# Another stored table for the order of issue in an attention and channel-mix kernel

## The chip, the cores and the metric

The kernel runs on one core of a Trainium2 chip. The metric is the device time of one execution in microseconds (us), the lower the better. A core has five engines that run beside each other, each with its own list of instructions, taken strictly in order: TensorE (PE, matrix products), VectorE (DVE), ScalarE (ACT), GpSimd (POOL), and SyncE (SP), which here issues all DMAs.

## What is computed

The reference is attention over pooled queries, followed by a channel mix; 8 batches, 8 heads, 1152 keys, 576 pooled queries, head size 64.

```
q_pool = q.reshape(B, H, S // 2, 2, D).mean(axis=3)
scores = q_pool @ k^T / sqrt(D); attn = softmax(scores); x = attn @ v    # x: (8, 576, 512)
x_prev = x moved by one position
xk = mu_k * x + (1 - mu_k) * x_prev;  xr = mu_r * x + (1 - mu_r) * x_prev
k = relu(xk @ w_k); v = (k * k) @ w_v; r = sigmoid(xr @ w_r); out = r * v
```

## The kernel before, in words

**Attention.** The 64 heads (8 batches of 8) are taken one after another, each in 6 blocks of 96 queries, 384 blocks in all (`block`, called at L808). A block uses one of three PSUM buffers `s0` to `s2` in turn and goes back and forth between the engines. PE computes 9 scores matmuls of 96 columns (L490, in two steps of 4 and 5). DVE takes the maximum over key chunks (L497). PE transposes it (L500), DVE takes the maximum again (L503), PE adds the correction (L505), ACT writes it into a row of the queries' low part (L508). PE runs 9 second scores matmuls on top (L514, two steps). ACT takes the exponential of all into `pf` (L520), and POOL cuts the low parts out of it (L523). With that the buffer is free for the block three further on. Where all queries of a stretch are there, `window` multiplies the weights with V: 9 pairs of hi matmuls (L549 and L551, 65 and 64 columns, in three steps) and 9 lo matmuls (L556, 65 columns, two steps) into one buffer `a`. After the head's last window DVE and ACT take `a` out (L573 to L580). For each head `prep` loads K and V, splits them into high and low halves (L433, L438, L457, L460, L463) and turns K by DMA (L449, L452); every second head `queries` does the like for two heads' queries (L388 to L416).

**Weights.** In the first 8 heads, batch 0, the weights of the channel mix, which come as 64-bit floats, are loaded (L630) and unpacked in 20 pieces by ACT (L638, L641, L653), DVE (L643, L645) and POOL (L654).

**Channel mix.** As soon as a batch's heads are through, `ff` runs over tiles of 256 positions, 18 in all: DVE and ACT mix x with its shifted copy (L686, L689, L695, POOL L697), and PE does 96 product matmuls of 256 columns and 72 of 512 columns for a tile (all at L717), with ACT (L744 to L770), POOL (L748) and DVE (L772, L781) between them and a store at the end (L784). Batch 0 and its successor's heads overlap: the products of a batch are issued between the blocks of the next one.

**The order.** No loop above issues anything at once. Each step is handed to `op` (`Issue.add`, L167) with its engine, a duration, and the buffers it reads and writes; one step can hold several matmuls. There are 5946 PE steps, 1590 for DVE, 1803 for ACT, 932 for POOL and 498 DMAs. `run` (L228) then reads the stored table `TURNS` (L50 to L141), one list for each engine, which says at each place how many of the engine's steps not yet issued are passed over. That alone sets the order on each engine:

```
for e in ENGINES:
    left = [n for n in range(len(ops)) if eng[n] == e]
    while left:
        ...
        order.append(left.pop(k + step))
```

`follow` (L194) plays these lists with the durations and the latencies `LAT` (L153), and the steps are put into the program by the times that come out; that sets how instructions of different engines stand against each other in the program, and nothing on one engine. The last lines of the kernel (L816 to L824) pin each engine's order.

Of the kernel before, what the change touches and what calls it, by code (L numbers as in the profile page):

```python
# [17 lines left out]
U8 = mybir.dt.uint8  # L18
# [4 lines left out]
P = 128  # L23
# [27 lines left out]
    "c-n<}349e*miMW8Rqxf?>+Nfjm*i#N6S9%8Z(#?CKxn~$ASjy(LR3Iha2v&_Ev+r?TQg2iI||y4wnDeltu`*LG#$j1j$?~}iX!}Qx${4_0y^K<-|"  # L51
    "sv3y{cPxU(WxWa~D!=I%%04B8B3V$k<3#)nqsr35SBQs7mCI$NgbHk<ah-l1b$9nl7IU9w!+NCy{QD<|W<lBMn6mX@=&}9Cp+0aR)VrL$ezp(}-$"
    "b-L5$(YPT7B%1^59wrQ%a#<fsL)AX38sV<uu4oAuDFdUwUL$NEmn<Dmr-EWUL?3xw{J0cq8JM&1>HO+`*kwrBk{E_rTG{2^j63%rPUWX%&%mL&M*"
    "&QjnJsx%;Q89&WPTj8S31^Bl)#g+S@;R?B7{iwu_mR`(bjG~Ngi|q;7#U8(88bX_d(2_?7EwgcC%eOAx5tpltrg_Q><$#|BVD)IVqQ*ecp~w*q54"
    "#NUY_9$k;CB*J9MvIr%*;_O~vdO8Lc3e;k@LH>Nc{eo=9%4l^c2UReL0tFan&H(Ce_vsx@g(*ikP<^YV1NU)Q7D2ju0P=zd&vs9rmTIVZV7s7Ke3"
    "5#y$7#Pf?em6KzUO~WMD)WT6)HNq>JDk>`LDk|!0I%{id5NxZiwpEptRa91tEGsLs*{Z6mY?YO^ilWlehN7aPnxbMjTh@lMvXm`?qrzbYxw)BKP+"
    "m5hn@jnWsmb7xN6DOIGL<YyrZUN{B;`?VI)`%7luAXTiD;Cf6p2tcNr?ph0g9TY8KR&czj)Mdl8+)D3Q;&n!9c+2B)8#o8!opC>{o=!3$ulUxzRv"
    "m)ubkf^0Snm$xr7c!{IcAK=D`zRRvK^GLcMB+%)xwmKTotLSdiJNB&UE7mcGW5sw;DT`tq*@_2o2m)os6{p9oc(+Zg1W5;wGy2Bv5-R1Ub9*@_f8"
    "7^15%hjqmooIsHlk#|ydZp%axg)L;w=3W>41_b!xLspnE*b?ka~K9W?BIS-p*@qI$yB4Y8CA_y)hrK8K}yNX!x-k|<mM#O2@u8Od2yn2C8Y?%lua"
    "h$@i@g0l8U4;Vy0$BqgoR+cx|>iGOIgPzlnZ%lnHJJ6WIYwHyY`jGR27|7)FQD(XiSu>NJNJ4RpB-Cj!AvjfQb9nhZvDy9`c<w&sJcY<8Q?hLQ|8"  # L60
# [189 lines left out]
def kernel(  # L250
# [219 lines left out]
    def block(n, j, i, t):  # L470
# [14 lines left out]
        def grid(c0, c1):  # L485
            return cols(c0, c1).rearrange("p (c q) -> p c q", q=QN)
# [368 lines left out]
```

## Time and profile before

| | us |
|---|---|
| median of 3 runs | 1116.58 (1115.95 to 1116.6) |
| the profiled execution, whole | 1115.82 |
| its span, first to last instruction | 1114.0 |
| busy: PE, DVE, ACT, POOL | 1077.0, 893.2, 842.0, 805.1 |

The profile is of one execution. Its span is 1.8 us shorter than that execution's own time, which is 0.8 us under the median. A busy PE in the profile is not PE at its peak, since matmuls overlap; the distance between the starts of two matmuls tells how fast it really goes. In the tables of windows the stretches are in us from the span's start, and PEclk is the share of full clock granted to TensorE, 1.00 for 2.4 GHz.

### The profile page before, as it was taken

How to read it: one execution, taken by the hardware profiler on the slowest of the kernel's cores; microseconds unless marked ns; L12 is line 12 of the kernel's file. 1: busy time of each engine (PE TensorE's matmuls, PEld its weight loads, DVE VectorE, ACT ScalarE, POOL GpSimd, SP SyncE). 2: the span in 40 equal slices, each digit the busy share in tenths (PEclk: the TensorE clock that was granted, in tenths of full speed). 3: DMA queues.
4: the chain of work that ended last, by engine and by line, in shares of the span. 5: the costliest groups of instructions: out<-in, count | busy, mean ns of one | idle time of the engine just before them, and what ended most of it. 6: DMA issues, size and time to landing. Idle time of an engine off the chain costs nothing.

```text
span 1114.0 us, 44713 instructions
## 1 busy us (share of the span) xinstructions
PE 1077.0 (97%) x18802; PEld 889.3 (80%) x18802; DVE 893.2 (80%) x1606; ACT 842.0 (76%) x1804; POOL 805.1 (72%) x940
## 2 busy tenths in 40 slices
PE   6888799999999999999999999999999999999998
PEld 5777687988788897988787888889797979787564
DVE  7999988898898898988787878787888889774321
ACT  6899987877878787878777786878777778765653
POOL 4778888877858787777777786868688777765431
PEclk9999999999999999999999999999999999999999
DMA  9999547675557654556455655565756354510000
GB/s 250 212 199 227 132 120 150 138 167 117 134 115 133 137 119 100 140 132 139 118 100 132 114 127 113 123 141 102 134 114 143 94 124 104 87 40 23 19 20 29
DMA packets 258153, 135.35 MB, mean 121 GB/s; under 512 B 193440, under 2 KB 230304, under 8 KB 257952
## 3 DMA queue, kind: packets, MB, share of 16 engines
q1 hardware_dynamic: 257952, 132.50, 54.4%
q8 instruction: 147, 2.41, 0.9%
q14 instruction: 54, 0.44, 0.1%
HBM read 67.11 MB, written 9.44 MB: 69 GB/s over the span
## 4 chain that ended last, share of the span: by engine, by line
PE 68%; DVE 1%; POOL 0%; DMA 0%; ACT 0%; issue 0%; POOLq 0%; DVEq 0%
PE f L717 28%; PE s L514 9%; PE s L490 9%; PE a L549 5%; PE a L551 5%; PE s L717 4%; PE a L556 4%; PE a L717 2%; PE s L500 1%; PE s L505 1%; DVE mx L497 0%; DMA kr<-in_k_dram 0%; DVE xr L689 0%; POOL pl L523 0%; DVE xk L689 0%
## 5 line engine op out<-in xcount | busy, mean ns | idle before, releaser
L497 DVE TENSOR_REDUCE mx<-s 128x96 f16<-128x864 f32 x384 | 399.6, 1052 | 83.5 <-PE s L490 43.2
L523 POOL TENSOR_SCALAR pl<-pf 128x864 f16<-128x864 uint16 (+1 forms) x384 | 332.8, 867 | 147.3 <-ACT pf L520 113.6
L520 ACT ACTIVATE pf<-s 128x864 int32<-128x864 f32 x384 | 335.2, 886 | 94.5 <-PE s L514 69.8
L549 PE MATMUL a<-vt,pf 128*128 128x65 f16 x2880 | 241.4, 194 | 0.6 <-DVE xb L580 0.4
L551 PE MATMUL a<-vt,pf 128*128 128x64 f16 x2880 | 241.8, 194 | 0.0
L490 PE MATMUL s<-qT,ks 128*128 128x96 f16 x3456 | 224.0, 208 | 10.1 <-ACT pf L520 8.1
L514 PE MATMUL s<-qT,ks 128*128 128x96 f16 x3456 | 215.8, 207 | 4.4 <-ACT qT L508 4.2
L490 PEld LDWEIGHTS <-ks 128*128 128x128 f16 x3456 | 184.4, 99 | 33.7 <-issue 12.2
L549 PEld LDWEIGHTS <-pf 128*128 128x128 f16 x2880 | 204.8, 98 | 5.1
L551 PEld LDWEIGHTS <-pf 128*128 128x128 f16 x2880 | 195.4, 98 | 8.2 <-issue 0.9
L514 PEld LDWEIGHTS <-ks 128*128 128x128 f16 x3456 | 179.7, 98 | 24.2 <-issue 5.5
L508 ACT ACTIVATE qT<-s 1x96 f16<-1x96 f32 x384 | 87.9, 233 | 77.1 <-PE s L505 73.2
L503 DVE TENSOR_REDUCE mb<-s 128x1 f16<-128x128 f32 x384 | 108.7, 286 | 37.1 <-PE s L500 32.9
L717 PE MATMUL f<-xhk,wk_hi 128*128 128x256 f16 x496 | 135.1, 272 | 0.5 <-DVE ex L645 0.5
L717 PE MATMUL f<-xlk,wk_hi 128*128 128x256 f16 x496 | 135.2, 272 | 0.1
L717 PE MATMUL f<-xhk,wk_lo 128*128 128x256 f16 x496 | 135.2, 272 | 0.0
L556 PE MATMUL a<-vb,pl 128*128 128x65 f16 x2304 | 126.6, 193 | 0.4 <-POOL pl L523 0.4
L717 PEld LDWEIGHTS <-wk_hi 128*128 128x128 f16 x1152 | 105.7, 98 | 14.9 <-issue 0.6
L556 PEld LDWEIGHTS <-pl 128*128 128x128 f16 x2304 | 101.0, 98 | 6.9 <-POOL pl L523 0.7
L748 POOL TENSOR_TENSOR gl<-g 128x512 f16<-128x512 f32 x72 | 77.0, 1071 | 40.4 <-ACT g L746 37.4
L438 POOL TENSOR_TENSOR kn<-kr,kn 128x320 f16<-128x320 f32 (+1 forms) x126 | 97.1, 785 | 5.9 <-ACT kn L433 1.8
L717 PE MATMUL f<-wv_lo,g 128*128 128x512 f16 x240 | 90.9, 379 | 0.0
(112 smaller groups left out, 2153.2 us busy)
## 6 DMA issues: line engine op xcount, KB each, us to landing
kr<-in_k_dram SPq DMA_DIRECT2D x64, 288.0 KB, 3.3
vr<-in_v_dram SPq DMA_DIRECT2D x64, 288.0 KB, 3.1
qr<-in_q_dram SPq DMA_DIRECT2D x32, 320.0 KB, 3.6
ks<-ks SPq DMA_DIRECT2D x64, 144.0 KB, 2.7
out_dram<-em SPq DMA_DIRECT2D x36, 256.0 KB, 2.3
qr<-in_q_dram SPq DMA_DIRECT2D x32, 256.0 KB, 3.3
st<-in_moe_w_k_dram SPq DMA_DIRECT2D x4, 512.0 KB, 6.0
xt<-in_moe_w_k_dram SPq DMA_DIRECT2D x4, 512.0 KB, 6.0
```

Source lines behind the costliest of these rows:

```text
L438: lambda cs=cs, en=nc.vector if ve else nc.gpsimd: en.tensor_tensor(kn[i][:, cs, D:P], kr[i][:, cs], kn[i][:, cs, 0:D], op=ALU.subtract),
L490: nc.tensor.matmul(cols(c, c + 1), ks1[hp][:, c, :], qhi, start=(c == c0), stop=False, skip_group_check=True)
L497: op("DVE", 0.967, lambda: nc.vector.tensor_reduce(mxz[:, P - QN:P], grid(0, NC).rearrange("p c q -> p q c"), axis=AX.X, op=ALU.max), r=[( ...
L503: op("DVE", 0.199, lambda: nc.vector.tensor_reduce(mbz, s[:, 0:P], axis=AX.X, op=ALU.max), r=[("s", z)], w=[("mb", z)], key=t + O_MAX)
L508: op("ACT", 0.15, lambda: nc.scalar.activation(qlo[0:1], s[0:1, 0:QN], AF.Prelu, scale=1.0 - EPS, alpha=(1.0 + EPS) / (1.0 - EPS)), r=[("s ...
L514: nc.tensor.matmul(cols(c, c + 1), ks2[hp][:, c, :], qlo, start=False, stop=True, skip_group_check=True)
L520: op("ACT", NC * QN / 1200 + 0.051, lambda: nc.scalar.activation(pf[:, :, HALF + rows.start:HALF + rows.stop], grid(0, NC), AF.Exp, bias=S ...
L523: op("POOL", NC * (r1 - r0) / 1000 + 0.066, lambda: nc.gpsimd.tensor_scalar(to, half(pf, U16, 0)[:, :, HALF + r0:HALF + r1], LO, 1.0, op0= ...
L549: nc.tensor.matmul(a_b[:, a0:a0 + VN], half(pf, F16, 1)[:, c, his], vt[jv][:, c, D:D + VN], start=(w == 0 and c == 0), stop=False, skip_gr ...
L551: nc.tensor.matmul(a_b[:, a0:a0 + D], half(pf, F16, 1)[:, c, his], vt[jv][:, c, 0:D], start=False, stop=(side and c == NC - 1), skip_group ...
L556: nc.tensor.matmul(a_b[:, a0:a0 + VN], pl[:, c, rows], vb[jv][:, c, 0:VN], start=False, stop=(c == NC - 1), skip_group_check=True)
L717: nc.tensor.matmul(ps, terms[i][0], terms[i][1], start=(first and i == 0), stop=(i == last), skip_group_check=True)
```

## The change

All of `TURNS` is replaced (91 lines by 91, the first and last of them below), and with it some durations and latencies that `follow` uses. The steps themselves, their instructions, shapes and buffers, are the same.

```diff
 TURNS = (
-    "c-n<}349e*miMW8Rqxf?>+Nfjm*i#N6S9%8Z(#?CKxn~$ASjy(LR3Iha2v&_Ev+r?TQg2iI||y4wnDeltu`*LG#$j1j$?~}iX!}Qx${4_0y^K<-|"
...
-    "Pm$l~ZnQ2xYE{{u{8&C>"
+    "c-nP(34j#E)&J|Bo|&GW`@VN)cV;h^z3*jNcDa|E-30_W)&oIZJOE{pO92nOAjTsq#&{dA_$dJ;p8=!MXi#H70Z*btO+W%7f<&$V@6{~I_x<y|n("
...
+    "KCPRPwui1{Pl<`=gcuCNqf0D%QaGtjuz3JEsxW)_uHEGs1YboGMXNmDQYiA?+{KWU%;2f_-X-T"
 )
...
-           ("ACT", "POOL"): 0.18, ("DVE", "POOL"): 0.155, ("POOL", "PE"): 0.11, ("ACT", "DVE"): 0.142,
-           ("DVE", "ACT"): 0.128, ("DVE", "DVE"): 0.12, ("ACT", "ACT"): 0.13, ("POOL", "POOL"): 0.13}
+           ("ACT", "POOL"): 0.18, ("DVE", "POOL"): 0.155, ("POOL", "PE"): 0.04, ("ACT", "DVE"): 0.142,
+           ("DVE", "ACT"): 0.128, ("DVE", "DVE"): 0.12, ("ACT", "ACT"): 0.13, ("POOL", "POOL"): 0.07}
...
-            op("DVE" if ve else "POOL", nn / 960 + 0.069 if ve else nn * 0.0020 + 0.11,
+            op("DVE" if ve else "POOL", nn / 960 + 0.069 if ve else nn * 0.0019 + 0.19,
...
-            op("PE", (c1 - c0) * 0.043, lambda c0=c0, c1=c1: scores(c0, c1),
+            op("PE", (c1 - c0) * 0.0425, lambda c0=c0, c1=c1: scores(c0, c1),
...
-            op("POOL", NC * (r1 - r0) / 1000 + 0.066, lambda: nc.gpsimd.tensor_scalar(
+            op("POOL", 0.93 if buf == ("pside",) else NC * (r1 - r0) / 1200 + 0.273, lambda: nc.gpsimd.tensor_scalar(
...
-            op("PE", 3 * 0.0595, lambda c0=c0: hi(c0, c0 + 3),
+            op("PE", 3 * 0.06, lambda c0=c0: hi(c0, c0 + 3),
...
-            op("PE", (c1 - c0) * 0.030, lambda c0=c0, c1=c1: lo(c0, c1),
+            op("PE", (c1 - c0) * 0.0322, lambda c0=c0, c1=c1: lo(c0, c1),
...
```

The other edited durations are of the same kind: the V low copy (0.67 to 0.75), the maximum (0.967 to 0.974), the transpose of the maximum (0.054 to 0.057), the correction (0.05 to 0.047), and the POOL and DVE steps of the turn, the weights and the mix.

Both tables can be read back to lists of steps. How they stand against each other (places moved, old list to new):

| engine | steps | on another place | mean move |
|---|---|---|---|
| PE | 5946 | 5573 | 9.2 |
| DVE | 1590 | 1443 | 5.4 |
| ACT | 1803 | 1591 | 4.6 |
| POOL | 932 | 707 | 2.0 |
| SP (DMA) | 498 | 388 | 2.2 |

And the number of steps in the lists up to and with a block's last step of a kind, old and new (blocks counted from 0 over all heads; 48 is the first of batch 1):

| block | PE, to L514 | of these products, in matmuls | DVE, to L503 | ACT, to L520 |
|---|---|---|---|---|
| 41 | 407, 400 | 0, 0 | 173, 177 | 187, 193 |
| 47 | 472, 459 | 0, 0 | 200, 199 | 214, 220 |
| 53 | 519, 551 | 6, 42 | 223, 226 | 244, 256 |
| 59 | 626, 650 | 82, 105 | 252, 252 | 278, 286 |
| 65 | 710, 757 | 124, 154 | 271, 283 | 306, 321 |
| 95 | 1157, 1150 | 312, 312 | 397, 393 | 438, 433 |

The first steps of ACT after the table load, old: mb, K cast 0, K cast 5, query cast 0, K copy, query cast 5, query copy (L412); new: mb, K cast 5, K cast 0, query cast 0, K copy, V copy 0, query copy (L412).

## Rows read from the trace of the kernel before

**Rows 1.** The page's first part: busy time in us, share and instructions of each engine.

```profile
PE 1077.0 (97%) x18802; PEld 889.3 (80%) x18802; DVE 893.2 (80%) x1606; ACT 842.0 (76%) x1804; POOL 805.1 (72%) x940
```

**Rows 2.** From the chain of waits that ended last, pieces in order of time: start in us, us, what; x is the number of matmuls run one behind the other.

```profile
487.98 0.77 PE s L514 x18
...
528.27 2.62 PE f L717 x24
...
539.75 2.59 PE f L717 x12
```

**Rows 3.** From the timeline of PE about 22.3 us: start in us, us of one, line and operation; the first and the last of twelve.

```profile
22.14 0.19 PE L549 MATMUL a<-vt,pf 128*128 128x65 f16 x1
...
22.47 0.19 PE L551 MATMUL a<-vt,pf 128*128 128x64 f16 x1
```

**Rows 4.** Groups of instructions by line, over the span: the count, busy us and mean ns of one, idle before them.

```profile
L551 PE MATMUL a<-vt,pf 128*128 128x64 f16 x2880 | 241.8, 194 | 0.0
L549 PE MATMUL a<-vt,pf 128*128 128x65 f16 x2880 | 241.4, 194 | 0.6 <-DVE xb L580 0.4 <-ACT xt L608 0.2
L490 PE MATMUL s<-qT,ks 128*128 128x96 f16 x3456 | 224.0, 208 | 10.1 <-ACT pf L520 8.1 <-ACT qT L412 1.7
L514 PE MATMUL s<-qT,ks 128*128 128x96 f16 x3456 | 215.8, 207 | 4.4 <-ACT qT L508 4.2
...
L556 PE MATMUL a<-vb,pl 128*128 128x65 f16 x2304 | 126.6, 193 | 0.4 <-POOL pl L523 0.4
```

**Rows 5.** Windows by stage: from:to, its length, busy us (x instructions) of PE, weight loads, DVE, ACT and POOL, then granted clock, DMA share, GB/s.

```profile
12.00:40.00 28.00, 23.27 (x450) 21.59 (x450) 22.80 (x45) 20.30 (x41) 16.34 (x20) 0.94 1.06 240
40.00:130.00 90.00, 73.14 (x1589) 65.39 (x1587) 86.31 (x165) 81.68 (x174) 70.78 (x83) 0.96 0.88 201
130.00:150.00 20.00, 17.72 (x328) 15.54 (x328) 18.29 (x31) 17.08 (x41) 17.02 (x22) 1.00 0.53 138
150.00:1080.00 930.00, 927.93 (x16217) 765.28 (x16215) 752.68 (x1336) 703.77 (x1515) 690.73 (x800) 1.00 0.52 112
1080.00:1114.00 34.00, 30.26 (x183) 17.71 (x181) 5.24 (x8) 11.72 (x20) 4.98 (x6) 0.97 0.08 31
```

**Rows 6.** The end of the chain of waits.

```profile
1110.30 0.69 DVE em L781
```

**Rows 7.** Timeline of ACT at the start.

```profile
7.29 0.63 ACT L391 ACTIVATE qn<-qs 128x512 f16<-128x512 f32 x1
7.82 0.68 ACT L412 COPY qT<-s 128x640 f16<-128x640 f16 x1
...
9.06 0.78 ACT L457 ACTIVATE vt<-vr 128x320 f16<-128x320 f32 x2
```

**Rows 8.** Groups of instructions of DVE and of ACT in 12:130, with what ended the idle time before them.

```profile
L497 DVE TENSOR_REDUCE mx<-s 128x96 f16<-128x864 f32 x50 | 51.7, 1049 | 4.8 <-PE s L490 3.0 <-ACT qn L391 0.8 <-ACT pf L520 0.4
L503 DVE TENSOR_REDUCE mb<-s 128x1 f16<-128x128 f32 x50 | 13.9, 284 | 2.4 <-PE s L500 2.3
...
L508 ACT ACTIVATE qT<-s 1x96 f16<-1x96 f32 x51 | 11.2, 231 | 5.6 <-PE s L505 5.4
```

**Rows 9.** Timeline of PE and of ACT about 13 us: one buffer's second scores, its exponential, and the scores that follow in it; in brackets the idle time before and what ended it.

```profile
12.81 0.91 PE L514 MATMUL s<-qT,ks 128*128 128x96 f16 x9
13.52 0.59 PE L505 MATMUL s<-negi,mb 128*128 128x96 f16 x2
14.70 0.88 PE L490 MATMUL s<-qT,ks 128*128 128x96 f16 x9 [0.59 <-ACT pf L520]
...
13.76 0.89 ACT L520 ACTIVATE pf<-s 128x864 int32<-128x864 f32 x1 [1.47 <-PE s L514]
```

**Rows 10.** Waits of PE in 135:1114, all of them: who waited for whom, us in total, times, longest.

```profile
PE s L514 <- ACT qT L508: 0.7, 2, 0.4
PE s L490 <- ACT pf L520: 0.6, 2, 0.4
PE s L505 <- DVE mb L503: 0.5, 2, 0.3
PE a L549 <- DVE xb L580: 0.4, 2, 0.2
PE a L556 <- POOL pl L523: 0.2, 1, 0.2
PE s L500 <- DVE mx L497: 0.2, 1, 0.2
```

**Rows 11.** Groups of the V subtraction in 12:130.

```profile
L460 DVE SCALAR_TENSOR_TENSOR vt<-vr,vt 128x320 f16<-128x320 f32 x8 | 4.4, 553 | 0.0
...
L460 DVE SCALAR_TENSOR_TENSOR vt<-vr,vt 128x256 f16<-128x256 f32 x8 | 3.2, 416 | 0.0
```

**Rows 12.** The same over the span.

```profile
L460 DVE SCALAR_TENSOR_TENSOR vt<-vr,vt 128x320 f16<-128x320 f32 x64 | 48.4, 756 | 0.0
...
L460 DVE SCALAR_TENSOR_TENSOR vt<-vr,vt 128x256 f16<-128x256 f32 x64 | 42.3, 662 | 0.0
```

**Rows 13.** Windows of 10 us, columns as in group 5.

```profile
30.00:40.00 10.00, 8.15 (x163) 7.55 (x163) 8.14 (x17) 8.31 (x17) 7.54 (x8) 0.83 1.01 235
50.00:60.00 10.00, 8.12 (x190) 7.22 (x188) 9.59 (x22) 8.46 (x20) 7.38 (x10) 1.00 1.06 275
110.00:120.00 10.00, 7.50 (x146) 6.90 (x143) 8.99 (x18) 8.02 (x17) 7.75 (x9) 0.83 0.92 197
```

More of the change, by code (lines that the diff above doesn't have):

```diff
@@ L56 @@
[L56 to L60, printed above, removed]
@@ new lines @@
+    "pbUuCA(A^?vW@E>g*?YN-TKEI|t8noOjsF`qve@cC2}_+8$xi+oN$Ig#uJPJV|^C#%Cw7OTZVHqyvMq?kytC=OjWljiVixMR0#Ufmk9+O&w9TxN?"
+    "&*EEwiK$=x^YBqCFQ%!0h5YjcXro}a6NeNs1R^6&ALB(RTP*}6rJQjz`60mBhM7Ds}LtI<uXG1|Xg^b^<#k8PmvZ-X%@pQ<cD^|r!A&b|dyDgf<Z"
+    "#HWd@_PMdi`i_BQUd*}VHJ-C&05l>g`yZoglq;<*lAOAg(6_X7xh}Kx*aT1*zWUzS4T2wv4l0VL({^k6!RV-XMx#c(o7-B(QPhW4`y^#wWJ(D-KO"
+    "hg51>m2X?cEG+X!1UO*8WH!WJu;&CZb7L@reg=5l36Fruq2JR1ZXR;xW=WlnvD#p=bAaZ5-}K-lazC(Y(Co;1{;3SQ--QC+pF0Semr(I6S<$F5<("
+    "7K=t27F5$zmDf@sCI!pIx$+96@<x=@mkungEiJ7st*Wl5tgNgUXEK$Ql$4l|ic5-%icEt|s9`D{U@A$c)0uRJaHQ3Il_)1&K$%PdrPGN-9>sGhCp"
@@ new lines @@
+    "RaSOjDHd^7B$D3RAc+UKq+`qO(FF3I;<#3I+xf`36Oz5!?+0f<X#E%6u-b%jM=ve*gmJBQJRjx7#ob2WtC~$VzTY#AUdg7N^5vhv-4_NYBNjYKde"
+    "#9w$;G(O4uB0ZX~jSWYr0sU*lB^ZWhba3t*WCW7RNdcEO@$E>A%W^_Vo%y6L#!|t#fe#2GmQr#Gai=0lyL3WE_Sa|7hNrv4B8HNoL?$#kfE=;m+7"
+    ";QuBMv+m(#aN3P&FaKxq6R9L7y)AnUy#k@GMP+vJJ6%rY^vU>+aM*XxkxS4)l31_4wTBt$w?&Ccp{#OQ$FRS@=}z_jpTrxcqB&AR5X$kP7)PIi6U"
+    "W2hX_*{2zdM+k4JMy0`71~)5t?^uZr=5C&MTzP;I1>Zgo)-lVwDVPMgg(p?|F4LDPmBWrk7G$~+jl&32B>rg6Dlvm0T%G1V|M6hM>!9lMrg#^$r3"
+    "RhDxeHcLagJe{AHr>0WKCzAz9HJwi7Q#vm{o{HzjS+7tmk5c7Pg@TD-Njw=(C=|u2_$h!z^Z8<0$Qw4hG$)bYTT$urs-A&7RW{6e+HNSolG8$VtP"
@@ L462, in prep @@
                r=[("vr", i), ("vt", j, c0)], w=[("vtl", j, c0)], key=key + 4, port=True)
-        op("POOL", 0.67, lambda: nc.gpsimd.tensor_scalar(
+        op("POOL", 0.75, lambda: nc.gpsimd.tensor_scalar(
             vb[j][:, :, 0:D], vr[i], SV, VLO, op0=ALU.mult, op1=ALU.mult),
@@ L493, in block @@
         for c0, c1 in BK:
-            op("PE", (c1 - c0) * 0.043, lambda c0=c0, c1=c1: scores(c0, c1),
+            op("PE", (c1 - c0) * 0.0425, lambda c0=c0, c1=c1: scores(c0, c1),
                r=[("ks1", hp, c) for c in (0, 5) if c < c1 and (c0 < 5 or c)] + kh, w=[("s", z)], key=t)
-        op("DVE", 0.967, lambda: nc.vector.tensor_reduce(mxz[:, P - QN:P], grid(0, NC).rearrange("p c q -> p q c"),
+        op("DVE", 0.974, lambda: nc.vector.tensor_reduce(mxz[:, P - QN:P], grid(0, NC).rearrange("p c q -> p q c"),
                                                          axis=AX.X, op=ALU.max),
            r=[("s", z)], w=[("mx", z)], key=t)
-        op("PE", 0.054, lambda: nc.tensor.matmul(s[:, 0:P], mxz, identb, start=False, stop=False,
+        op("PE", 0.057, lambda: nc.tensor.matmul(s[:, 0:P], mxz, identb, start=False, stop=False,
                                                  skip_group_check=True),
@@ L504, in block @@
            r=[("s", z)], w=[("mb", z)], key=t + O_MAX)
-        op("PE", 0.05, lambda: nc.tensor.matmul(s[:, 0:QN], mbz.broadcast_to([P, P]),
+        op("PE", 0.047, lambda: nc.tensor.matmul(s[:, 0:QN], mbz.broadcast_to([P, P]),
                                                  negi[:, P - QN:P], start=False, stop=False, skip_group_check=True),
@@ L517, in block @@
         for c0, c1 in BK:
[L518 removed]
+            op("PE", (c1 - c0) * 0.0425, lambda c0=c0, c1=c1: scores2(c0, c1),
                r=[("ks2", hp)] + kl, w=[("s", z)], key=t + O_EXP)
@@ L588, in window @@
                r=[("xb", 0), ("xb", 1)], w=[("xbh",), *old[0]], key=t + O_TURN)
-            op("POOL", NW * P * 0.0019 + 0.09, lambda: nc.gpsimd.tensor_tensor(xbl, xz.rearrange(flat), xbh, op=ALU.subtract),
+            op("POOL", NW * P * 0.0019 + 0.2, lambda: nc.gpsimd.tensor_tensor(xbl, xz.rearrange(flat), xbh, op=ALU.subtract),
                r=[("xb", 0), ("xb", 1), ("xbh",)], w=[("xbl",), *old[0]], key=t + O_TURN)
@@ L593, in window @@
                    r=[(kx,)], w=[(kx, "t"), *old[1]], key=t + O_TURN, tail=1.6)
-            op("POOL", TQ * 0.0019 + 0.09, lambda: nc.gpsimd.tensor_tensor(
+            op("POOL", TQ * 0.0019 + 0.2, lambda: nc.gpsimd.tensor_tensor(
                 xt[b % 3][:, g, 1:1 + TQ], xth[:, HALF:], xtl[:, HALF:], op=ALU.add),
@@ L653, in weights @@
                 op("ACT", 0.52, lambda hi=hi, e=e: nc.scalar.copy(hi, e), r=[ke], w=[("w", n, c, f)], key=key)
-                op("POOL", 1.13, lambda lo=lo, e=e, hi=hi: nc.gpsimd.tensor_tensor(lo, e, hi, op=ALU.subtract),
+                op("POOL", 1.18, lambda lo=lo, e=e, hi=hi: nc.gpsimd.tensor_tensor(lo, e, hi, op=ALU.subtract),
                    r=[ke, ("w", n, c, f)], w=[("wl", n, c, f)], key=key)
@@ L688, in mix @@
    r=xk + [("omu", w)], w=[("tmp", z)], key=key + c * dk)
-                op("DVE", ln / 960 + 0.069, lambda x=x, s0=s0, ln=ln, o0=o0, z=z, c=c: nc.vector.scalar_tensor_tensor(
+                op("DVE", ln / 960 + 0.13, lambda x=x, s0=s0, ln=ln, o0=o0, z=z, c=c: nc.vector.scalar_tensor_tensor(
                     xm[w][:, c, o0:o0 + ln], x[:, c, s0 + 1:s0 + 1 + ln], m[:, c:c + 1], tmp[z][:, 0:ln],
@@ L696, in mix @@
                    r=[("x", w, c, False), ("x", w, c, True)], w=[("xh", c)], key=key + c * dk)
-            op("POOL", n * 0.0019 + 0.09, lambda c=c: nc.gpsimd.tensor_tensor(
+            op("POOL", n * 0.0019 + 0.2, lambda c=c: nc.gpsimd.tensor_tensor(
                 xl[w][:, c, 0:n], xm[w][:, c, 0:n], hi[:, c, 0:n], op=ALU.subtract),
@@ L747, in ff @@
                 g32[:, f2, 0:n], r32[z][:, :, 0:n], AF.Square), r=[("r32", z)], w=[("g", f0)], key=key + 1)
-            op("POOL", 2 * n * 0.0018 + 0.1, lambda f2=f2: nc.gpsimd.tensor_tensor(
+            op("POOL", 2 * n * 0.0018 + 0.14, lambda f2=f2: nc.gpsimd.tensor_tensor(
                 gl[:, f2, 0:n], g32[:, f2, 0:n], gh[:, f2, 0:n], op=ALU.subtract),
```

162 lines of the change are left out of this document (78 added, 84 removed).

## The prediction

> **What bounds the kernel now.** First the page's first line [rows 1]: TensorE (PE) is busy 1077.0 of 1114.0 us, VectorE (DVE), ScalarE (ACT) and GpSimd (POOL) 72 to 80%. A busy PE may still be waiting inside, so the second step is its bare work, from the distance between starts in the chain of work and in the timeline at full clock. Eighteen scores matmuls take 0.77 us, 0.0428 each; twenty-four 256-column products 2.62, 0.109 each; twelve 512-column products 2.59, 0.216 each [rows 2]; a 65-column matmul starts 0.030 after the one before (11 distances from 22.14 to 22.47) [rows 3]. Counts times these: 3456 + 3456 scores 295.8; 2880 + 2880 + 2304 window matmuls 241.9 [rows 4]; 18 tiles x 96 products of 256 columns 188.4 and 18 x 72 of 512 columns 279.9; 384 max transposes (128 columns) and 384 corrections (96), by columns from the scores, 38; 3 for transposes. The sum is 1047 us. No order can go below that with its start and end, so all that a new order can touch is some 67 us.
>
> The windows by stage tell where they lie [rows 5]. In 150:1080 PE is busy 927.9 of 930. In 12:150 it is busy 114.1 of 138. In 40:130 DVE is busy 86.3 of 90 and ACT 81.7, PE 73.1: here DVE sets the pace, because batch 0 has no channel-mix products yet to fill PE, and the weights are unpacked on DVE and ACT beside its 48 blocks. From 150 on PE sets the pace. A new order gains where PE comes sooner to its full stage, and loses where it makes PE wait after that. The tail is fixed: the last gate product runs on DVE for 0.69 us from 1110.30 [rows 6], and then the store.
>
> **The change part by part.** The planner's new durations and latencies cost nothing of themselves: an engine's order is read from the table alone, and they only place the engines' instructions against each other in the program. All the weight is in the table, which I decoded for both kernels; counts of steps below are from the two decoded lists, prices from rows.
>
> Start. ACT's sixth step, the cast of the second part of the queries (0.53 us from its start at 7.29 to the next at 7.82), now stands behind the query copy that the first scores wait for, and a V copy of 0.39 us (0.78 for two) stands in its place [rows 7]. Its V load moves from fifth to third on SP's queue; the copy ran at 9.06 with no wait, and has until 7.29. Value -0.14 at most; I take -0.2 with the smaller half of K first; ends 0 and -0.5 (the 0.53 whole).
>
> The stage set by DVE. Up to the end of block 53 the new lists have 3 more DVE steps (two mixes, one reduction), 12 more ACT steps and 32 more PE steps: 36 product matmuls (36 x 0.109 = 3.9), 48 hi matmuls of windows and 9 lo matmuls (57 x 0.030 = 1.7), 18 scores matmuls (0.8), 6.4 us of PE work done sooner. By the page's means [rows 1] the DVE steps cost 3 x 893.2/1606 = 1.7 us and the ACT steps 12 x 842.0/1804 = 5.6 us. If DVE alone keeps the pace, block 53 ends 1.7 us later with 6.4 more of PE done: gain 4.7. If ACT becomes the pace: 0.8. In 40:130 DVE idles 3.7 us and ACT 8.3 [rows 5], so ACT has room for its 5.6 and DVE has none: I take 4.7. A check six blocks on, at block 59: DVE the same 252 steps, PE 24 more, worth 23 x 0.109 + 18 x 0.030 + 27 x 0.030 and two small ones, 4.0. The further end is above: in 12:130 DVE idles 4.8 us before maxima and 2.4 before second maxima [rows 8]; if the order closes half of that, 3.6 more; nothing in the counts shows it, so it is in the range alone. POOL's 707 moved steps of 932 and SP's 388 of 498 move by 2.0 and 2.2 places in the mean; POOL is busy 70.8 of 90, so no term of its own.
>
> The stage set by PE. Four chains per block leave PE and come back: scores to maximum, maximum to second maximum, correction to second scores, second scores through the exponential to the scores three blocks on in the same buffer. The last, bare: nine second scores start at 12.81, the next PE step at 13.52; the exponential starts at 13.76 and the scores at 14.70, after a wait for it [rows 9]. So 1.18 us from the one's end must be covered by other PE work: 0.24 to its start, 0.89 for it, 0.05 back. With the same two hops and the means of their own steps (1049, 284 and 231 ns [rows 8]) the other three need 1.34, 0.57 and 0.52. Counted in PE work by the prices above over blocks 60 to 383, the median cover of this chain falls from 1.61 to 1.41, and that of correction to second scores from 1.08 to 0.90. Against the bare chains the shortages add up to 2.1 us in the old table and 4.0 in the new. The old 2.1 stands beside 2.6 us of PE waits measured after 135 us [rows 10], so this reckoning is near, and I take the difference, +1.9. Below: nothing or a gain of 2.6, all waits gone. Above: each chain 0.10 us longer than bare (another step in its way), 3.8 against 8.5, so +4.7; 0.15 longer, 5.1 against 15.6, +10.5.
>
> SP's queue. K and V loads lose some lead: the shortest PE work between what frees the buffer and what needs the load falls from 8.6 to 7.4 us. Cover enough: 0; a load that is late once would cost about the missing part of that, under 1.2.
>
> Sum: -0.2 - 4.7 + 1.9 = -3.0 on the profiled execution's 1115.82, so 1112.8; the median of the runs shown is 0.8 above it, so **1113.6**. About 0.2% (2.2 us) is what a measurement of this kernel can tell from no change.
>
> **The rivals.** Tight covers (slower). The place is blocks 60 to 383, the price is the shortage above; it decides beyond a margin of some 0.12 us per chain, where the added waits pass 7.1. At 0.15: -0.2 - 4.7 + 10.5 = +5.6, **1122.2**. For it: 83 covers of the exponential's chain are shorter than bare plus 0.15, against 12. Against: in the old trace only 2.6 us were waited at all, and a wait of PE gives the other engines the time to come ahead, so not every shortage is paid. Chance 0.20.
>
> The gain is given back. The products of batch 0 are finite: both tables have the same 312 matmuls of products ahead of block 95's second scores, so the 3.9 us used sooner are missing between blocks 53 and 95. If DVE or ACT then sets the pace again, the stage's 4.7 is lost: +1.7, **1118.3**. Against: in 150:1080 DVE is busy 752.7 of 930 [rows 5]. Chance 0.13.
>
> DVE slowed by POOL. The V subtraction (L460, both inputs in SBUF) takes 553 and 416 ns in 12:130 and 756 and 662 over the run [rows 11, 12]. Moved against POOL's steps, the 8 + 8 of that stretch could take the longer times: 8 x 0.203 + 8 x 0.246 = 3.6 us of DVE, gain 1.1, **1117.2**. Chance 0.07. The Trainium skill (GPSIMD Engine Reference, Specifications) says that GpSimd's SBUF interfaces are shared with VectorE, and that instructions of VectorE with two SBUF inputs contend; the two lengths of L460 agree with that.
>
> PE's clock. It was granted at 0.83 in 30:40 and in 110:120, with PE busy 8.15 and 7.50 of 10, and at 1.00 in 50:60 with 8.12 [rows 13]; a fall costs up to 10 x 0.17 = 1.7 us. Three more falls before block 50, where the new order has 1.2 to 2.2 us less PE work ahead of blocks 41 and 47, would cost 5.1: +2.1, **1118.7**. Against: PE waits for DVE there, and a slower matmul fills a wait. Chance 0.03. The Trainium skill (TensorE: Matmul & The Clock Gate, HAM oscillation) has it that idle gaps of PE lower its clock, which speaks against moving PE work out of this stretch; the trace has falls in it, but also the same idleness without one.
>
> DVE's idle closed. Half of 7.2 more: -6.6, **1110.0**. Chance 0.12. That the change does nothing is excluded: 5573 of 5946 PE steps change place.
>
> **How the numbers follow.** The forecast has 0.45, of which 0.40 lies beyond 0.2%. Faster: 0.40 + 0.12 = 0.52. Within: 0.05 + 0.13 + 0.07 + 0.03 = 0.28. Slower: 0.20. The range goes from 1106.5 (all of DVE's 7.2 closed: 1113.6 - 7.2 = 1106.4) to 1119.5 (the three middle rivals inside, the tight covers at a margin over 0.12 outside). The forecast's own range is 1111 to 1116.
>
> **What would show it.** Right: in 40:130 PE is busier than 73.1 at a DVE still above 86; product matmuls by block 53's end; PE full from some 145 us on; PE's waits after 150 a few us, on the exponential (L520) above all. Wrong: waits of 8 us or more there (tight covers); a stretch near 200 to 250 where PE drops below 98% (given back); L460 above 600 ns in 12:130 (POOL); more stretches at 0.83 (clock). The forecast is wrong if the time is above 1114.4, and its reason is wrong if the gain lies behind 150 us.

## The result: slower, and the profile after

| | us | mean granted clock of TensorE |
|---|---|---|
| before, median of 6 runs | 1115.92 (1114.09 to 1116.6) | 0.995 in the profiled one |
| after, median of 6 runs | 1123.57 (1120.26 to 1127.08) | 0.983 to 0.991 |
| ratio, 95% interval | 1.0071 (1.0057 to 1.0086) | |
| after, the profiled execution | 1120.26, span 1118.4 | 0.991 |

The change costs 7.65 us where a gain of 3.0 was forecast. The profiled execution is the fastest of the six, 4.4 us above the one of before, and it has the highest clock of the six. At the other end 1127.08 us goes with 0.983: about 0.85 us for each 0.001 of clock. Two executions of some 2.8 ms, one of before beside e1 to e4 and one of e12, are left out of all medians, ratios and counts of runs here.

Busy time from the page of after, beside [rows 1], with the row of the clock in 40 slices:

```profile
PE 1081.2 (97%) x18802; PEld 890.8 (80%) x18802; DVE 874.3 (78%) x1606; ACT 838.9 (75%) x1804; POOL 804.9 (72%) x940
...
PEclk9889899999999999999999999999999999999999
```

The same instructions, 4.2 us more of busy PE, 19 less of DVE. The clock is short of full in the first 150 us alone. The windows by stage answer to [rows 5]:

```profile
12.00:40.00 28.00, 24.47 (x462) 22.65 (x463) 24.37 (x47) 21.20 (x43) 16.15 (x20) 0.88 0.97 242
40.00:130.00 90.00, 70.17 (x1533) 62.14 (x1529) 83.71 (x160) 82.49 (x177) 71.42 (x83) 0.95 0.79 196
130.00:150.00 20.00, 19.83 (x333) 17.93 (x333) 12.98 (x26) 14.97 (x35) 15.25 (x20) 0.88 0.50 116
150.00:1080.00 930.00, 927.27 (x16239) 764.50 (x16236) 737.25 (x1339) 698.32 (x1512) 689.06 (x798) 1.00 0.54 112
1080.00:1118.40 38.40, 34.68 (x205) 19.77 (x202) 7.15 (x11) 14.46 (x25) 7.32 (x9) 1.00 0.07 28
```

In 40:130 neither PE nor DVE is busier: 70.2 and 83.7 where before had 73.1 and 86.3, so the prediction's first sign of being right is missing. PE does have its products sooner, 19.8 of 20 busy in 130:150, but at a clock of 0.88. Windows of 10 us show where the clock fell, as [rows 13]:

```profile
30.00:40.00 10.00, 8.92 (x178) 8.31 (x177) 8.82 (x16) 8.36 (x17) 7.68 (x9) 0.70 0.80 235
60.00:70.00 10.00, 6.79 (x184) 6.50 (x182) 9.69 (x19) 8.27 (x17) 7.69 (x9) 1.00 0.72 221
70.00:80.00 10.00, 8.12 (x119) 7.05 (x119) 9.10 (x20) 8.90 (x21) 6.19 (x8) 0.66 0.98 224
120.00:130.00 10.00, 7.93 (x181) 6.77 (x180) 8.96 (x17) 8.90 (x21) 8.58 (x11) 0.91 0.35 65
130.00:140.00 10.00, 9.83 (x106) 8.24 (x106) 6.82 (x14) 7.21 (x18) 6.97 (x10) 0.75 0.39 104
```

By the clock records PE ran at 1.2 GHz for 6.8 us each from 29.2, 70.1 and 128.2: 20.4 us. In the profile of before it was 3.4 us each from 33.7, 98.5 and 115.6: 10.2. PE was busy only 6.79 of the 10 us ahead of 70.

What PE waited for up to 135 us (us in total, times, longest):

```profile
PE s L500 <- DVE mx L497: 8.6, 16, 1.0
PE s L514 <- ACT qT L508: 6.2, 11, 2.6
...
PE a L605 <- ACT xhk L695: 1.7, 1, 1.7
PE a L549 <- issue: 1.5, 1, 1.5
```

The waits of 2.6 and 1.7 us end just as two of the falls begin. In PE's timeline, block 24's second scores (the first block of a new pair of heads) and the first of the transposes of x (L605):

```profile
70.16 0.88 PE L514 MATMUL s<-qT,ks 128*128 128x96 f16 x9 [2.65 <-ACT qT L508]
...
127.84 0.58 PE L605 MATMUL a<-ident,xb 128*128 128x128 f32 x3 [1.72 <-ACT xhk L695]
```

ACT's timeline tells why the first is late: L508 of block 24 stands in ACT's new list behind two weight steps, and the second of them waits for DVE.

```profile
67.71 0.66 ACT L641 ACTIVATE xt<-xt 128x512 int32<-128x512 uint8 x1
69.32 0.63 ACT L638 ACTIVATE f<-xt 128x512 f32<-128x512 f32 x1 [0.95 <-DVE ex L645]
69.88 0.22 ACT L508 ACTIVATE qT<-s 1x96 f16<-1x96 f32 x1
```

The tail kept its length. The last L781, at 1110.30 in [rows 6], stands 4.42 us later in the chain of waits, which is all of the difference of the profiled spans:

```profile
1114.72 0.69 DVE em L781
```

To follow the loss along the run I use one number, the **lag** of a block: the start of its last second scores, less the bare time of all PE work ahead of it in the list. Bare is the distance between starts at full clock (0.0426 us for 96 columns, 0.0294 for 64 and 65, 0.056 for 128, 0.109 for 256, 0.216 for 512; about 0.031 for the lo matmuls of L556 and 0.11 for the transposes of x); fillers, below, are not counted as work. Lag is what PE has lost so far by waits or by a slow clock, and it allows for work done sooner.

| lag in us at block | 24 | 51 | 57 | 95 | 383 | us at half clock up to 150 |
|---|---|---|---|---|---|---|
| before | 29.6 | 53.6 | 56.3 | 56.9 | 65.2 | 10.2 |
| after | 31.6 | 57.3 | 57.5 | 59.2 | 69.7 | 20.4 |
| e2: new order, then old | 32.6 | 61.6 | 61.8 | 63.5 | 72.8 | 34.0 |
| e5: new order, waits filled | 30.7 | 53.8 | 54.0 | 56.0 | 67.1 | 0 |
| e8: e2, waits filled | 31.0 | 54.9 | 55.1 | 57.1 | 66.4 | 3.4 |
| e11: old order, some waits filled | 29.9 | 52.1 | 55.8 | 56.4 | 64.8 | 3.4 |

### The profile page after: what moved, and what is told of

It reads as the page before. It is cut to its first block, busy times and chain, and to the rows that moved or that the text cites. A ratio compares the mean times of both kernels' runs of the same rounds, so it can differ in the third digit from the quotient of the medians.

```text
span 1118.4 us, 44635 instructions
## 1 busy us (share of the span) xinstructions
PE 1081.2 (97%) x18802; PEld 890.8 (80%) x18802; DVE 874.3 (78%) x1606; ACT 838.9 (75%) x1804; POOL 804.9 (72%) x940
## 4 chain that ended last, share of the span: by engine, by line
PE 88%; DVE 5%; ACT 3%; issue 2%; DMA 0%; DVEq 0%; ACTq 0%
PE f L717 35%; PE s L514 12%; PE s L490 12%; PE a L549 7%; PE a L551 7%; PE a L556 6%; PE s L717 4%; DVE mx L497 2%; PE s L500 2%; PE a L717 2%; PE s L505 2%; ACT pf L520 1%; DVE mb L503 1%; DVE f L643 1%; DVE ex L645 0%
## 5 line engine op out<-in xcount | busy, mean ns | idle before, releaser
L520 ACT ACTIVATE pf<-s 128x864 int32<-128x864 f32 x384 | 336.9, 886 | 104.1 <-PE s L514 80.0
L549 PE MATMUL a<-vt,pf 128*128 128x65 f16 x2880 | 241.1, 193 | 2.0 <-issue 1.5
L490 PE MATMUL s<-qT,ks 128*128 128x96 f16 x3456 | 226.7, 208 | 6.0 <-ACT pf L520 3.9
L514 PE MATMUL s<-qT,ks 128*128 128x96 f16 x3456 | 221.5, 208 | 7.3 <-ACT qT L508 6.7
L490 PEld LDWEIGHTS <-ks 128*128 128x128 f16 x3456 | 185.7, 99 | 30.7 <-issue 8.2
L549 PEld LDWEIGHTS <-pf 128*128 128x128 f16 x2880 | 203.7, 98 | 6.8 <-issue 1.6
L514 PEld LDWEIGHTS <-ks 128*128 128x128 f16 x3456 | 182.7, 99 | 26.8 <-issue 9.2
L503 DVE TENSOR_REDUCE mb<-s 128x1 f16<-128x128 f32 x384 | 108.8, 287 | 48.5 <-PE s L500 42.8
L508 ACT ACTIVATE qT<-s 1x96 f16<-1x96 f32 x384 | 87.6, 231 | 68.9 <-PE s L505 62.1
L717 PE MATMUL f<-xhk,wk_hi 128*128 128x256 f16 x496 | 135.6, 273 | 0.1
L717 PE MATMUL f<-xlk,wk_hi 128*128 128x256 f16 x496 | 135.6, 273 | 0.0
L717 PE MATMUL f<-xhk,wk_lo 128*128 128x256 f16 x496 | 135.5, 273 | 0.0
L556 PE MATMUL a<-vb,pl 128*128 128x65 f16 x2304 | 128.8, 193 | 0.0
L717 PEld LDWEIGHTS <-wk_hi 128*128 128x128 f16 x1152 | 106.1, 98 | 13.9 <-issue 0.2
L556 PEld LDWEIGHTS <-pl 128*128 128x128 f16 x2304 | 103.3, 98 | 8.6
L438 POOL TENSOR_TENSOR kn<-kr,kn 128x256 f16<-128x256 f32 (+1 forms) x126 | 95.5, 768 | 8.7 <-ACT kn L433 3.6
L500 PE MATMUL s<-identb,mx 128*128 128x128 f16 x384 | 84.2, 222 | 9.4 <-DVE mx L497 8.8
```

The source lines that it names most:

```text
L438: lambda cs=cs, en=nc.vector if ve else nc.gpsimd: en.tensor_tensor(kn[i][:, cs, D:P], kr[i][:, cs], kn[i][:, cs, 0:D], op=ALU.subtract),
L490: nc.tensor.matmul(cols(c, c + 1), ks1[hp][:, c, :], qhi, start=(c == c0), stop=False, skip_group_check=True)
L500: op("PE", 0.057, lambda: nc.tensor.matmul(s[:, 0:P], mxz, identb, start=False, stop=False, skip_group_check=True), r=[("mx", z)], w=[("s" ...
L503: op("DVE", 0.199, lambda: nc.vector.tensor_reduce(mbz, s[:, 0:P], axis=AX.X, op=ALU.max), r=[("s", z)], w=[("mb", z)], key=t + O_MAX)
L514: nc.tensor.matmul(cols(c, c + 1), ks2[hp][:, c, :], qlo, start=False, stop=True, skip_group_check=True)
L520: op("ACT", NC * QN / 1200 + 0.051, lambda: nc.scalar.activation(pf[:, :, HALF + rows.start:HALF + rows.stop], grid(0, NC), AF.Exp, bias=S ...
```

## The experiments

The theories at the start were that the loss comes from the first two batches (late queries at blocks 24 and 48, a falling clock), or from tight covers after them. The runs of before made beside the experiments had medians of 1115.4 to 1116.1. The runs of the old order with an edit (e4, e6, e11) have the old table in the kernel of after, so with its planner's durations; these were not run by themselves.

**e1 and e2: which part of the table.** A step taken from the one order was taken with all that it rests on.

```diff
 TURNS (e1)
-  all steps in the new order
+  steps that before starts ahead of 248.6 us (block 95): in the old order; then the rest in the new
 TURNS (e2)
-  all steps in the new order
+  steps that after starts ahead of 249.5 us: in the new order; then the rest in the old
```

> The old order up to the end of batch 1 (248.6 us in the old trace, block 95), then the new one. If the loss lies in the first two batches (late steps, clock): within 3 us of before, 1114 to 1119. If it lies in the tight covers of blocks 60 to 383: most of the 7.6 us lost stays, 1120 to 1124.

> The new order up to the end of batch 1 (249.5 us in the new trace), then the old one. If the loss lies in the first two batches: slow as the new table, 1119 to 1124, with its wide spread between runs and a granted clock under 0.992. If in the tight covers: 1113 to 1118 with a clock of 0.995.

Measured: e1 1119.74, ratio 1.0035 (1.0022 to 1.0048), clock 0.994 to 0.996; e2 1124.53, ratio 1.0081 (1.0068 to 1.0094), clock 0.983 to 0.985. e1 lies between its two ranges, e2 just above its first and without the wide spread (1123.37 to 1125.76). Both parts lose. e1 has nearly the clock of before (one fall of 3.4 us more in its profile, at 135.3), so most of its loss lies behind its join: its lag grows by 11.4 us from block 95 to 383, where that of before grows by 8.3. e2 has the slowest clock of all. Its windows (40 to 130, and 90 to 100 us):

```profile
40.00:130.00 90.00, 74.16 (x1516) 67.28 (x1513) 80.03 (x151) 78.71 (x167) 66.97 (x77) 0.87 0.75 192
...
90.00:100.00 10.00, 7.73 (x103) 6.76 (x100) 8.21 (x15) 7.71 (x17) 8.49 (x10) 0.59 0.89 248
```

Up to 249 us e2 and after run the same lists, yet e2 is 4.3 us further behind at block 95 (63.5 against 59.2), with 13.6 us more at half clock: 0.32 us lost for each us at half clock. The spread of after's own runs says about the same: 0.001 of mean clock over 1122 us is 2.24 us at half clock, and went with 0.85 us, 0.38 for each.

**e3 and e4: more PE work in every block.**

```diff
         def scores(c0, c1):
-            for c in range(c0, c1):
+            for c in [*range(c0, c1)] * (2 if i < 54 else 1):
```

> The new order, with the first scores matmuls of blocks 0 to 53 run twice (the second run overwrites the first): 9 x 0.043 = 0.39 us more PE work a block, 21 us in all, where PE waits for DVE. If falls of PE's clock are what costs: no fall after 20 us, and 1114 to 1119 in spite of the work. If the clock is only a sign of the waits: 1122 to 1130, the chain of a block being 0.39 us longer.

> The old order with the same doubled scores. If the clock costs the old order too (falls at 33.7, 98.5 and 115.6 us in its trace): 1111 to 1115. If the clock is only a sign: 1116 to 1122.

Measured: e3 (new order) 1130.86, ratio 1.0138 (1.0123 to 1.0153), clock 0.995 to 0.997; e4 (old order) 1125.89, ratio 1.0088 (1.0075 to 1.0101), clock 0.997 to 0.999. The window 40 to 130 of e3, then of e4:

```profile
40.00:130.00 90.00, 77.97 (x1784) 72.57 (x1781) 76.46 (x145) 77.26 (x161) 65.82 (x75) 0.96 0.79 199
```

```profile
40.00:130.00 90.00, 77.45 (x1846) 72.26 (x1843) 80.94 (x153) 76.66 (x163) 66.40 (x76) 1.00 0.83 189
```

The clock came back but for one fall each (6.8 us from 78.9 in e3, 3.4 from 144.6 in e4), and both times lie above all ranges given for them. The 21 us of work cost 7.3 and 10.5 us: work put into a block's own chain is in part paid, though PE waits in this stage. DVE fell to 76.5 and 80.9 of 90, so DVE's total alone doesn't set the pace; the chain of a block through PE, DVE and ACT counts too. On the clock these runs decide nothing: gain and cost are mixed.

**e5, e6 and e8: fill the waits alone.** Here no step moves. Each of PE's waits of over 0.4 us between 20 and 131 us, where a place free of readers could be found, gets small matmuls that run while PE would wait.

```diff
+WARM = {341: (0, 4), 349: (1, 5), ... 656: (2, 30), ... 1092: (0, 20), ...}
...
+            if n in WARM:
+                self.warm(*WARM[n])
             ops[n][2]()
...
+    iss.warm = lambda z, k: [nc.tensor.matmul(a_b[:, 384:512] if z == 3 else s_b[z][:, 992:1024],
+        identb, identb[:, 0:128 if z == 3 else 32], start=False, stop=False, ...) for _ in range(k if z == 3 else 2 * k)]
```

> The new order, with small extra matmuls (identity by identity, into columns of PSUM that nothing reads) put only into TensorE's waits of over 0.4 us between 20 and 131 us, each filling some 60% of its wait (11.4 us of them in 27 places); no step moves. Theory C: the loss is TensorE's clock. The runs of before have a mean granted clock of 0.994 to 0.996, those of the new order 0.983 to 0.991, and among the new order's own runs 0.001 of clock goes with about 0.85 us (1127.08 at 0.983, 1120.26 at 0.991). Filled waits then bring the clock back to 0.995 or more and the time to 1115 to 1118. Rival O: the new lists lose the time by the waits themselves, and the low clock only comes with them: the clock may come back, but the time stays at 1120 or above. Rival N: the clock doesn't answer to such matmuls: clock under 0.992, time 1121 to 1127.

> The order of before with its own waits of over 0.4 us between 20 and 131 us filled in the same way (10.6 us in 28 places). C: its three half-clock stretches of 3.4 us go, clock 0.998 or more; at 1.0 to 1.3 us for each 0.001 (its own runs: 1116.5 at 0.994, 1114.0 at 0.996) the time falls to 1110 to 1113. O and N: 1115 to 1117, as before.

> New order to 249.5 us and the old one after it (1124.53 without fillers, clock 0.985), with the fillers of e5. C: clock 0.995 or more, and what is left is the gain of the products issued sooner (about 2.5 us by the lag of blocks 51 to 57) without the later waits of the new order (about 2 us): 1111 to 1114, the fastest of this call or beside the filled old order. O: 1120 or above.

Measured: e5 1117.64, ratio 1.0022 (1.0012 to 1.0033), clock 0.998 to 1.000; e6 1117.40, ratio 1.0022 (1.0012 to 1.0031), clock 0.995 to 0.998; e8 1115.45, ratio 1.0004 (0.9996 to 1.0013), clock 0.998 to 1.000. The windows of e5 up to 1080 us:

```profile
12.00:40.00 28.00, 24.64 (x538) 22.70 (x539) 25.73 (x47) 22.12 (x46) 16.82 (x21) 1.00 1.04 244
40.00:130.00 90.00, 77.55 (x1822) 69.88 (x1819) 84.44 (x163) 83.04 (x178) 72.00 (x84) 1.00 0.83 202
130.00:150.00 20.00, 19.74 (x358) 18.11 (x358) 16.67 (x28) 16.55 (x37) 16.93 (x22) 1.00 0.53 110
150.00:1080.00 930.00, 926.68 (x16194) 762.60 (x16193) 736.52 (x1335) 695.25 (x1506) 687.21 (x796) 1.00 0.54 112
```

The clock is full in all of them, and no step was moved. The new order gains 5.9 us by it (1123.57 to 1117.64), and e2's order 9.1 (1124.53 to 1115.45): this is theory C. The old order, which had less to get back, loses 1.6, so fillers are no gain of their own. C's forecasts for e6 (1110 to 1113) and e8 (1111 to 1114) missed: these fillers also cost something, as e10 to e12 show with fewer. With its waits filled the new order is within 0.3 us of the old. Between e5 and e8, which share the fillers and the order up to 249.5 us, the new order after that costs 2.2 us.

**e7: shorten the longest wait.**

```diff
 ACT's list about block 24
   L573 (window)
+  L508 (block 24)
   L641 (weights)
   L638 (weights)
-  L508 (block 24)
   L391 (queries)
```

> The new order with one step moved: ACT's L508 of block 24 goes ahead of two weight steps (L641 and L638), which stand before it in the new list and of which the second waits 0.95 us for DVE. TensorE's wait of 2.65 us before block 24's second scores should fall to about 0.5. If that wait brings on the half clock at 70 to 77 us (6.8 us), the stretch goes or gets shorter, the clock rises by about 0.003 and the time falls by 2 to 3 us to 1120.5 to 1121.5; if the fall comes from the poor start of the head as a whole, the stretch stays and the time is 1122 to 1124.

Measured: 1124.18, ratio 1.0079 (1.0062 to 1.0096), clock 0.983 to 0.994: nothing gained. In its profile block 24's wait was 0.49 in place of 2.65 us, but block 25's was 2.98 in place of 0.54, since its L508 still stands behind the weight steps and the queries in ACT's list. And 70 to 80 us had the same low clock (half of full for 6.8 us from 71.2, in the middle of that wait):

```profile
69.25 0.54 PE L514 MATMUL s<-qT,ks 128*128 128x96 f16 x9 [0.49 <-ACT qT L508]
...
72.78 0.88 PE L514 MATMUL s<-qT,ks 128*128 128x96 f16 x9 [2.98 <-ACT qT L508]
```

```profile
70.00:80.00 10.00, 6.44 (x95) 5.63 (x95) 9.06 (x20) 8.23 (x18) 5.09 (x7) 0.66 0.78 203
```

So the edit moved the long wait by one block and did not shorten it; whether such a wait brings on the fall is not shown either way.

**e9 and e10: the new order only to block 58.**

```diff
 TURNS (e9, e10)
-  all steps in the new order
+  steps that after starts ahead of 151.7 us: in the new order; then the rest in the old
+WARM = e5's 27 waits (e9); 15 of them, about the falls (e10)
```

> The new order only to the start of block 58 (151.7 us), the order of before for the rest, with the same 27 fillers as e5. If the new lists gain what they gain by block 57 (in e5 the stretch ahead of block 57's second scores is 2.3 us shorter than in before at full clock) and lose it after that (1.4 us more than before between blocks 57 and 95, and some 2.7 us more after block 95), this order keeps the gain: 1112.5 to 1114.5, faster than before. If the fillers or the join hide a cost of their own, 1115 to 1117 as e8.

> The order of e9 with fillers in only 15 waits, those of the stretches in which TensorE worked least ahead of a fall (7.0 to 7.8 us of filler in place of 11.4). If the fillers cost time of their own, faster than e9 by up to 1 us with the clock still at 0.997 or more: 1112 to 1114; if the clock falls again in the stretches left out, 0.993 to 0.996 and 1114 to 1117.

Measured: e9 1116.31, ratio 1.0007 (0.9998 to 1.0016), clock 0.998 to 1.000; e10 1115.03, ratio 0.9998 (0.9989 to 1.0006), clock 0.996 to 0.998. e9 came out in the second of its ranges, and e10 1 us above its first. The lead was gone at the join (the lag at block 57 is 55.8 in e9, where e5 has 54.0), so the gain of the first part was not had without the lists that follow it. Fewer fillers are better, by 1.3 us.

**e11 and e12: few fillers, both whole orders.**

```diff
+WARM = 11 waits about the three falls of before (e11, old order)
+WARM = e10's 15 waits (e12, new order)
```

> The order of before with fillers in 11 waits ahead of its three half-clock stretches alone (4.5 us of filler, where e6 had 10.6 us in 28). If e6's fillers ate the gain of its clock (1117.4 at 0.998, where before runs 1115.8 at 0.995), this shows it: clock 0.998 or more and 1112.5 to 1115. If half clock costs the old order nothing, 1115.5 to 1116.5 at any clock.

> The whole new order with the 15 fillers of e10 alone. C: nearly all of the clock is back (0.996 to 0.999) and the fillers left out gave nothing but their own cost, so the time is that of e5 less 0 to 1 us: 1116.5 to 1118; beside e11 (the old order with its few fillers, 1115.17 at 0.998) the new order is then 1.5 to 2.5 us slower at the same clock, which is about what its lists lose after 95 us. If the clock still falls (0.99 to 0.995): 1118 to 1121. If the order were faster once the clock holds: 1113 to 1115.

Measured: e11 1115.17, ratio 0.9990 (0.9982 to 0.9999), clock 0.997 to 1.000; e12 1115.84 in ten runs, ratio 1.0003 (0.9994 to 1.0012), clock 0.995 to 0.998. e11 came out 0.2 us above its first range; it is the only kernel of this study whose interval lies below 1, barely, at about 0.1%. e12, the whole new order, came out 0.7 us below the range that theory C gave it: 1.8 us under e5, where at most 1 was expected. At nearly the same clock it stands 0.7 us above e11 by the medians, and 1.5 by the ratios, each to the runs of before beside it. PE's timeline of e12 where after waited 2.65 us, with the fillers (L346) in the wait (this execution is the slowest of the ten, and still has half clock for 3.4 us from 70.9 and for 6.8 from 115.3):

```profile
65.69 1.66 PE L346 MATMUL s<-identb 128*128 128x32 f16 x60
68.52 0.54 PE L514 MATMUL s<-qT,ks 128*128 128x96 f16 x9 [1.17 <-ACT qT L508]
```

## Why the prediction was wrong

**PE's clock: the step that failed.** It had no term in the sum and stood as the least likely rival, at 0.03, with the argument that PE waits there anyway and a slower matmul fills a wait. Its price was near: 1.7 us a fall in the prediction, against 0.32 us for each us at half clock between e2 and after, 1.1 for a fall of 3.4 us. Its number was not: three more falls were the rival, which is what the profiled execution has, counted in stretches of 3.4 us; but that is the fastest of six. A mean clock of 0.9863 over the six runs, at some 1122 us, makes 2 x 0.0137 x 1122 = 31 us at half clock, against some 11 at 0.995 in before: 20 more, or about 6 such stretches. And the argument was wrong. A wait is not idle time to be filled by slowness: the matmuls that come after it belong to the chain of a block, and each of them at half clock is that much later for DVE and ACT. A us at half clock can cost at most 0.5 us of work, and 0.32 was paid. Filling the waits takes nearly all of the loss away: the new order falls by 7.7 us (1123.57 to 1115.84 in e12), the old one by 0.75 (1115.92 to 1115.17 in e11), with clocks of 0.995 to 0.998 and 0.997 to 1.000. So 7.0 of the 7.65 us go with the clock, and 0.7 are left to the lists (by the ratios 6.5 and 1.5), give or take what the fillers themselves cost. The price says the same: 20 us more at half clock, at 0.32 each, are 6.4.

The Trainium skill (TensorE: Matmul & The Clock Gate, HAM oscillation) has idle gaps of TensorE lower its clock. The runs agree in this: with its gaps filled e5 has 1.00 in every window. The prediction named the rule and gave it too little weight.

**The stage set by DVE: -4.7 forecast, mis-sized.** The counts were right, and PE is in its full stage sooner: from block 51 to 57 the lag of before grows by 2.7 us, that of after and e5 by 0.2. But DVE's total alone does not set the pace (e3 and e4, where it fell well under 86 of 90 and the time rose), so more work per DVE step is not a gain of its own. Ahead of that the new order is slower at the first blocks of two pairs of heads: from block 23 to 24 the lag of e5 grows by 2.9 us and that of e11 by 0.7, from 47 to 48 by 3.9 and 1.8, and at block 51 e5 has 53.8, e11 52.1. At block 57 the gain is 54.0 against 55.8, 1.8 us; at block 95 56.0 against 56.4, 0.4. The 1.8 is no clean number: the one fall left in e11, at 133.1, lies in this stretch and makes about 1.0 of it, and e5's larger number of fillers may hide some gain. What was done sooner is **given back** by block 95, the rival that had 0.13. Its place was right, but the amount is 1.4 and not 4.7, and its mechanism is shown in part alone: PE's few waits there are for DVE and ACT (0.8 us in e5, 146 to 250 us), but PE is busy 50.0 of 50 us in 200:250 of after, where the sign was under 98%.

**The stage set by PE: +1.9 forecast, right in size and mostly in its chain.** From block 95 to 383 the lag grows by 8.3 in before and 8.4 in e11; in after 10.5, in e1 11.4, in e5 11.1. So +2.2 to +3.1. The waits of PE after 135 us fell, from 2.6 us in [rows 10] to 1.9; the longest row of after is now the exponential's:

```profile
PE s L490 <- ACT pf L520: 0.8, 3, 0.4
```

What rose most is in the queue of weight loads, which the prediction didn't read. Between 250 and 1030 us, in before and then in after:

```profile
PEld L505 <- DVE mb L503: 2.0, 6, 0.6
PEld L500 <- DVE mx L497: 1.1, 4, 0.5
```

```profile
PEld L500 <- DVE mx L497: 4.7, 20, 0.4
PEld L490 <- issue: 1.9, 6, 0.6
...
PEld L505 <- DVE mb L503: 0.8, 3, 0.3
```

All waits of this queue that the view lists rose by 4.1 us, from 5.0 to 9.1, which is more than PE lost, so they don't price the loss. The lag does, split by the line that starts late. Of the 2.2 us more in after from block 95 to 383, the scores (L490) have +1.6, transposition (L500), windows (L549) and products (L717) +0.7, +0.7 and +0.4, other lines together -1.2. In each of the eight late starts of L490 (by 0.13 us or more), an exponential had ended 0.05 us before, the hop of [rows 9]. So the exponential's chain, which the prediction named above all, lost most, and the first chain, scores to maximum (20 waits of weight loads in place of 4), came second with the windows. In e8, with the old lists after 249.5 us, the row is that of before:

```profile
PEld L500 <- DVE mx L497: 1.1, 4, 0.5
```

**The rival of tight covers** (0.20, 1122.2) gave a time near the measured one, by the wrong mechanism: the waits of PE that it needed, 8 us or more after 150 us, are not there.

**DVE slowed by POOL.** In 12 to 130 us, beside [rows 11]:

```profile
L460 DVE SCALAR_TENSOR_TENSOR vt<-vr,vt 128x320 f16<-128x320 f32 x7 | 4.3, 617 | 0.0
...
L460 DVE SCALAR_TENSOR_TENSOR vt<-vr,vt 128x256 f16<-128x256 f32 x7 | 3.0, 435 | 0.0
```

These are longer by 64 and 19 ns: 7 x 0.064 + 7 x 0.019 = 0.6 us, of 3.6 that the rival priced. **SP's queue and the start** show no loss; the lag at block 3 is 13.8 in after, 14.5 in before.

So the sum nearly without the clock (e5 against e11) is -1.8 up to block 57, +1.4 from there to 95, +2.7 from there to 383: +2.3 by the lags of these two profiled executions, +3.3 without e11's one fall, and +0.7 by the medians of e12 and e11 (+1.5 by the ratios), where -3.0 was forecast. The clock is the rest. What stays open is which feature of the new lists lets it fall more: e7 only moved the longest wait by a block, and I tried no other. How much of the 0.7 to 1.5 is the fillers' own cost is open too.

## What to carry to other kernels

Before an order is priced by counts and durations, read the granted clock of each stretch and the runs' clocks beside their times: a stage in which TensorE waits for others has a price per us at half clock, and a new order can raise the number of such us without moving any total. One profiled execution does not show how often the clock falls; several runs with their clocks do. Where the clock is suspected, fill the waits without moving a step, and compare both orders so filled. Take what a stage loses from the distances between PE's starts, line by line: here PE's own waits fell and the weight loads' rose by more than PE lost. And look in the trace at whether an edit that was to shorten a wait has only moved it.

## What the runs showed of the hardware

Matmuls of 32 and 128 columns whose result nobody reads, 11 us of them in 27 waits, held TensorE at 2.4 GHz (mean clock 0.998 to 1.000 in eight runs of e5) through a stage in which it otherwise had 20 to some 38 us at 1.2 GHz (0.991 to 0.983 in after). In the old order, 11 places with 4.5 us of them brought 0.995 to between 0.997 and 1.000.

TensorE also stopped with nothing to wait for that the profile shows, mostly in mid-group, once or twice for 0.2 to 1.7 us, in the profiles of after and of all runs but e1, e2 and e11, and not in that of before. The row of after, then of e3 and of e4:

```profile
99.90 0.20 PE L549 MATMUL a<-vt,pf 128*128 128x65 f16 x1 [1.50 <-issue]
```

```profile
30.50 0.20 PE L549 MATMUL a<-vt,pf 128*128 128x65 f16 x1 [1.11 <-issue]
```

```profile
29.32 0.25 PE L556 MATMUL a<-vb,pl 128*128 128x65 f16 x3 [1.41 <-issue]
```

The 1.5 us of after are part of the lag of after between blocks 33 and 39. The Trainium skill (Runtime: NRT & Kernel Launch, Instruction fetch mechanics) says that each engine's instructions come in blocks by a DMA queue of its own, at a cost that is mostly hidden; a block that comes late would look like this, but no run here shows that it was one.
